# Attention followed by a max-out MoE on one core: unchained token transposes, a new query layout, one PSUM bank per job kind, and a token ring with a shorter tail

## The chip, the cores and the metric

The kernel runs on one core of a Trainium2 chip. The metric is device time in microseconds (us), the median of several executions. The profile is one execution with the hardware profiler; its span runs some 2 us below that same execution's time. So kernels of the same job are compared first, and small differences between jobs are treated with care.

## The reference, cut to what matters

```python
def _attn_ref(q, k, v):                       # q, k, v: (8, 8, 1152, 64)
    q_pool = q.reshape(B, H, S // 2, 2, D).mean(axis=3)
    scores = scale * np.matmul(q_pool, k.transpose(0, 1, 3, 2))
    attn = softmax(scores)                    # shortened here
    return np.matmul(attn, v)                 # (8, 8, 576, 64)

def _moe_ref(x, w1, w2, w_out):               # x: 4608 tokens x 512
    g = np.maximum(x @ w1, x @ w2)            # 1024 columns
    return g @ w_out
```

The kernel uses max(h1, h2) = h2 + relu(h1 - h2). It keeps w1 - w2 ("wd") and w2 @ w_out ("w21"). For each block of tokens it computes relu(x wd) (the "h" jobs, result in `gT`) and then x w21 + gT w_out (the "p" jobs).

## The kernel before

Two heads of a batch form a pair, and there are 32 pairs. For each pair the SP queue loads q, k and v. POOL casts k and v and pools q. TensorE (PE) forms the scores, ACT takes the exponentials (`eta`, `etb`), PE multiplies them by v, and DVE normalizes into `xnat`. After four pairs (one batch, 576 tokens) five DMA transposes put `xnat` into `xT`, and MoE work on these tokens may start.

A small planner in Python (`Plan`, with estimated costs) decides the static order of all instructions, and each engine executes its list in that order. PSUM holds three double banks for the scores and two single banks, `fb[0]` and `fb[1]` ("lanes"), for everything else.

`w` names what an operation writes, and `under` names the weights that once lay where `xT` is now written:

```python
def xtrans(b):
    for j in range(NCH + 1):
        ...
        under = [key for key, lo, hi in (("w2b", 512, 1536), ("w2T", 1536, 2560),
                                         ("w2f", 2560, NTOK))
                 if n0 < hi and lo < n0 + rows]
        op("SP", lambda e, ...: e.dma_start_transpose(
            xT[:, :, n0:n0 + rows], xnat[xs][0:rows, j, :]),
            r=[f"xn{xs}.{j}.{h}" for h in range(H)],
            w=[f"xT.{b}.{j}"] + under,        # every transpose "writes" w2f ...
            dma=f"d_x{xs}{j}", cost=0.95, mode="t")
```

Because each transpose writes the key `w2f` (or `w2T`, `w2b`), each one waits until its predecessor has landed, although they touch different columns. Loads, k transposes and stores of results share the in-order SP queue with them. A p job's bank becomes free when DVE has copied it to one of three output buffers `osb`, and such a buffer becomes free when its store has landed.

The lanes were filled without distinction:

```python
def refill():
    if q_queue and ...: return q_queue.pop(0)      # query and key transposes
    if av_queue and ...: return av_queue.pop(0)[0] # attention times v
    if w_queue and ...: return w_queue.pop(0)      # weights
    ... # then MoE; a p job only when no h job is in a lane
```

The softmax here doesn't subtract the row's maximum and nothing guards it: scores larger than these inputs give would overflow.

## Time and profile before

| what | before |
|---|---|
| median time | 435.13 us (432.31 to 435.33) |
| span of the profile | 438.0 us |
| PE busy / ACT busy | 388.1 us / 313.1 us |
| mean granted PE clock | 0.967 |
| PE waiting for an output copy (`DVE stage`) | 11.2 us in 8 waits |
| SP queue waiting for a token transpose | 47.1 us in 26 waits |

The profiled execution took 439.74 us, more than any of the three timed ones of its job and 1.7% above the fastest of them. So the sums of this trace lie on the high side.

These lines are from the page of the kernel before: busy time by engine, then the 40 slices of PE and of the granted clock in tenths, then the chain that ended last by engine and by line.

```profile
PE 388.1 (89%) x4714; PEld 205.9 (47%) x4765; DVE 152.7 (35%) x351; ACT 313.1 (71%) x365; POOL 130.4 (30%) x104
...
PE   2879969799999998799989997999869999999995
...
PEclk9999995889999999899999999999989999999999
...
PE 64%; DMA 15%; DVE 7%; ACT 6%; SPq 3%; issue 2%; POOL 1%; DVEq 0%
```

PE is the engine that is nearly always busy, and the chain runs mostly through it. But 15% of the chain is DMA, which should be hidden. (The loads of weights number 4765 and the matmul records 4714: some 50 matmuls are missing from this trace, so PE busy is a little too low. PE busy is therefore not compared to better than some us.)

The window table of the kernel before shows where PE stands still. Its columns are the stretch, its length, busy time of PE, weight loads, DVE, ACT and POOL (with counts), granted clock, DMA share and GB/s.

```profile
60.00:70.00 10.00, 5.41 (x34) 1.74 (x32) 6.20 (x8) 4.16 (x5) 1.32 (x2) 0.72 1.10 222
170.00:180.00 10.00, 6.48 (x88) 4.28 (x90) 1.75 (x3) 4.24 (x5) 0.00 (x0) 0.85 0.70 184
280.00:290.00 10.00, 9.73 (x139) 5.47 (x139) 4.74 (x11) 9.31 (x12) 4.71 (x4) 1.00 1.07 274
310.00:320.00 10.00, 6.59 (x54) 2.26 (x52) 0.69 (x1) 7.23 (x9) 4.08 (x3) 1.00 1.06 311
320.00:330.00 10.00, 8.61 (x126) 5.99 (x127) 4.50 (x11) 4.38 (x5) 4.07 (x3) 0.83 1.14 274
```

A good window (280 to 290) has PE at 9.7 and ACT at 9.3 of 10 us. A hole (310 to 320) has PE at 6.6, and the window after it a clock of 0.83.

The chain of the kernel before, in order of time, around that hole (start, length, what; a few entries are left out at the dots):

```profile
295.37 2.43 DMA xT<-xnat
297.79 0.01 issue
297.81 2.43 DMA xT<-xnat
...
300.26 2.40 DMA xT<-xnat
302.66 0.02 issue
302.68 4.47 DMA xT<-xnat
307.15 0.02 issue
307.16 1.17 SPq L435
...
310.01 2.31 SPq L256
...
313.05 6.94 DMA out_dram<-stage
...
320.09 0.70 DVE stage L587
320.79 0.05 issue
320.83 3.37 PE fb L333 x63
```

Read it downwards. The transposes go one after the other. Behind them in the SP queue come the loads, a k transpose and at last a store. When the store has landed, DVE may copy the next output. Only then is a PSUM bank free and PE goes on with attention, after 4.24 us of standing still. The 63 matmuls that follow take 3.37 us where the same 63 take 2.08 us at 161.67 us. Two lines of PE's timeline show it:

```profile
161.67 2.08 PE L333 MATMUL fb<-vE,eta 128*128 128x65 bf16 x63 [0.53 <-DVE stage L587]
320.83 3.37 PE L333 MATMUL fb<-vE,eta 128*128 128x65 bf16 x63 [4.24 <-DVE stage L587]
```

The clock had been halved: the window table gives 0.50 from 321 to 323 us. The Trainium skill (TensorE: Matmul & The Clock Gate, Part 1) says that an idle window of about 3.4 us halves it, and this hole agrees.

The waits of PE and of the SP queue on it (total us, times, longest):

```profile
PE fb L333 <- DVE stage L587: 11.2, 8, 4.2
...
PE sps L394 <- ACT eta L406: 6.1, 15, 0.7
PE sps L394 <- DMA kT<-kbf: 3.9, 1, 3.9
PE fb L541 <- DVE rc L357: 3.7, 7, 0.9
PE fb L571 <- DVE rc L357: 3.1, 5, 1.2
```

```profile
SPq L435 <- DMA xT<-xnat: 47.1, 26, 8.2
```

### The profile page before, as it was taken

What the parts mean: (1) busy time and instruction counts of PE and PEld (TensorE: products, weight loads), DVE (VectorE), ACT (ScalarE), POOL (GpSimd) and SP (SyncE); (2) the same over time, 40 slices, a digit from 0 to 9 for tenths busy, and PEclk for the clock granted to TensorE, in tenths of its full rate; (3) what the DMA queues carried; (4) which work ended last, traced back from release to release, by engine and by line L of the source; (5) the groups of instructions that cost most, each with busy time, mean ns of one, the idle gap of its engine ahead of it and who ended that gap; (6) DMA issues with size and microseconds to landing.
All of it is one profiled execution on the core that took longest, in us unless ns stands there. A gap on an engine that the chain in (4) does not pass through costs nothing.

```text
span 438.0 us, 10776 instructions
## 1 busy us (share of the span) xinstructions
PE 388.1 (89%) x4714; PEld 205.9 (47%) x4765; DVE 152.7 (35%) x351; ACT 313.1 (71%) x365; POOL 130.4 (30%) x104
## 2 busy tenths in 40 slices
PE   2879969799999998799989997999869999999995
PEld 1446535544554442555455554554345454633442
DVE  2246443234334412334243331442235233443121
ACT  1999948979897988499929995898829977601121
POOL 3733425265303451333045404450244201000000
PEclk9999995889999999899999999999989999999999
DMA  8999999899749994997599839982899634023213
GB/s 233 306 350 341 256 290 255 158 304 277 136 93 250 268 262 80 257 280 146 128 323 238 206 79 313 294 211 49 207 283 281 117 87 124 3 48 102 49 48 96
DMA packets 83648, 85.74 MB, mean 196 GB/s; under 512 B 54417, under 2 KB 54417, under 8 KB 83601
## 3 DMA queue, kind: packets, MB, share of 16 engines
q1 hardware_dynamic: 83600, 85.05, 78.0%
q8 instruction: 37, 0.61, 0.6%
q14 instruction: 11, 0.08, 0.1%
HBM read 62.91 MB, written 9.44 MB: 165 GB/s over the span
## 4 chain that ended last, share of the span: by engine, by line
PE 64%; DMA 15%; DVE 7%; ACT 6%; SPq 3%; issue 2%; POOL 1%; DVEq 0%
PE fb L571 17%; PE fb L333 15%; PE sps L394 13%; PE fb L541 13%; ACT eta L406 6%; DMA xT<-xnat 4%; DMA kT<-kbf 4%; PE fb L344 4%; DMA qraw<-in_q_dram 3%; DMA out_dram<-stage 3%; DVE stage L555 2%; DVE xnat L361 2%; DVE stage L587 1%; SPq L256 1%; SPq L435 1%
## 5 line engine op out<-in xcount | busy, mean ns | idle before, releaser
L406 ACT ACTIVATE eta<-sps 128x1024 bf16<-128x1024 f32 x288 | 270.1, 1051 | 62.6 <-PE sps L394 62.1
L394 PE MATMUL sps<-qpT,kT 64*128 64x64 bf16 (+1 forms) x1152 | 108.0, 298 | 12.5 <-ACT eta L406 6.1
L333 PE MATMUL fb<-vE,eta 128*128 128x65 bf16 x2304 | 97.0, 199 | 11.9 <-DVE stage L587 11.2
L333 PEld LDWEIGHTS fb<-vE,eta 128*128 128x128 bf16 x2304 | 86.5, 101 | 37.8 <-DVE stage L587 12.4
L249 POOL TENSOR_SCALAR kbf<-kraw 128x1152 bf16<-128x1152 f32 x31 | 35.7, 1150 | 159.7 <-DMA kraw<-in_k_dram 159.7
L541 PE MATMUL fb<-xT,wd 128*128 128x512 bf16 x259 | 68.8, 384 | 6.6 <-DVE rc L357 3.7
L262 POOL TENSOR_TENSOR qp<-qraw 96x768 bf16<-96x768 f32 x32 | 57.8, 1806 | 46.8 <-DMA qraw<-in_q_dram 37.0
L571 PE MATMUL fb<-wo,stage 128*128 128x512 bf16 x281 | 70.7, 380 | 0.9 <-issue 0.8
L555 DVE TENSOR_SCALAR stage<-fb 128x512 bf16<-128x512 f32 x64 | 43.3, 689 | 56.6 <-PE fb L541 56.6
L394 PEld LDWEIGHTS sps<-qpT,kT 64*128 64x128 bf16 x1152 | 30.5, 95 | 66.2 <-ACT eta L406 38.3
L587 DVE COPY stage<-fb 128x512 f32<-128x512 f32 x32 | 21.8, 690 | 104.5 <-PE fb L571 95.3
L418 ACT ACTIVATE etb<-sps 128x1024 bf16<-128x1024 f32 x64 | 39.2, 678 | 10.6 <-PE sps L394 10.1
L270 POOL TENSOR_SCALAR vE<-vraw 128x1152 bf16<-128x1152 f32 x32 | 36.8, 1149 | 26.0 <-PE sps L394 16.6
L571 PEld LDWEIGHTS fb<-wo,stage 128*128 128x128 bf16 x288 | 25.1, 98 | 36.6 <-issue 11.9
L541 PEld LDWEIGHTS fb<-xT,wd 128*128 128x128 bf16 x288 | 22.3, 98 | 37.3 <-issue 5.1
L571 PE MATMUL fb<-w,xT 128*128 128x512 bf16 x132 | 35.3, 380 | 4.3 <-DVE rc L357 3.1
L357 DVE RECIPROCAL rc<-fb 128x6 f32<-128x6 f32 (+1 forms) x64 | 12.1, 189 | 74.1 <-PE fb L344 54.9
L361 DVE TENSOR_TENSOR xnat<-fb,rc 128x256 bf16<-128x256 f32 x64 | 27.2, 425 | 2.2
L550 ACT ACTIVATE stage<-fb 128x512 bf16<-128x512 f32 x8 | 4.8, 597 | 28.2 <-PE fb L541 28.2
L344 PE MATMUL fb<-vE,etb 128*128 128x131 bf16 x288 | 22.6, 224 | 0.0
L289 PE MATMUL fb<-ident,qp 96*128 96x96 bf16 x192 | 14.6, 216 | 8.6 <-POOL qp L262 7.9
L571 PEld LDWEIGHTS fb<-w,xT 128*128 128x128 bf16 x144 | 11.4, 97 | 21.9 <-DVE xnat L373 4.1
(27 smaller groups left out, 109.0 us busy)
## 6 DMA issues: line engine op xcount, KB each, us to landing
qraw<-in_q_dram SPq DMA_DIRECT2D x32, 576.0 KB, 9.4
kraw<-in_k_dram SPq DMA_DIRECT2D x32, 576.0 KB, 7.5
vraw<-in_v_dram SPq DMA_DIRECT2D x32, 576.0 KB, 10.3
out_dram<-stage SPq DMA_DIRECT2D x24, 192.0 KB, 3.2
out_dram<-stage SPq DMA_DIRECT2D x24, 128.0 KB, 4.3
xT<-in_moe_w_dram SPq DMA_DIRECT2D x1, 2048.0 KB, 15.6
stage<-in_moe_w_out_dram SPq DMA_DIRECT2D x1, 2048.0 KB, 22.3
stage<-in_moe_w_dram SPq DMA_DIRECT2D x1, 2048.0 KB, 21.9
```

What stands on the lines that cost most here:

```text
L249: op("DVE" if i == 0 else "POOL", lambda g: g.tensor_scalar(kbf[s][:, :, :, :].rearrange("p t h d -> p h t d"), kraw[s][:, :, :, :], 1.0, ...
L262: op("POOL", lambda g: g.tensor_tensor(qp[s][:, :, :, :].rearrange("p u h d -> p h u d"), qraw[s][:, :, :, 0, :], qraw[s][:, :, :, 1, :], ...
L270: op("POOL", lambda g: g.tensor_scalar(vE[v3][:, :, :, 0:D].rearrange("p t h d -> p h t d"), vraw[s][:, :, :, :], 1.0, 1.0, ALU.mult, ALU. ...
L333: last = e.matmul(fb[m][:, sb * 66:sb * 66 + 65], eta[es][:, half, t, sb * P:(sb + 1) * P], vE[vs][:, t, half, 0:65], start=(t == 0), stop ...
L344: last = e.matmul(fb[m][:, 4 * 66:4 * 66 + 131], etb[es][:, t, :, :].rearrange("p h c -> p (h c)"), vE[vs][:, t, :, :].rearrange("p h c -> ...
L361: dve(lambda e: e.tensor_tensor(xnat[xs][:, 0:NCH, c:c + D], a[:, 0:NCH * 66].rearrange("p (j c) -> p j c", c=66)[:, :, 0:D], rc[half][:, ...
L394: return e.matmul(sps[r][:, half, col:col + n], kT[ks][h:h + 64, t, :], qpT[qs][h:h + 64, lo:lo + n], start=True, stop=True)
L406: return e.activation(eta[es][:, :, g, :], sps[r][:, :, :], EXP, scale=scale)
L418: return e.activation(etb[es][:, t0:t0 + n, :, :].rearrange("p t h c -> p h t c"), sps[r][:, :, 0:n * NB].rearrange("p h (t c) -> p h t c" ...
L541: last = e.matmul(fb[m][:, :], wd[:, ct, ft * P:(ft + 1) * P], xT[:, ct, n0:n0 + 512], start=(ct == 0), stop=(ct == NC_ - 1))
L555: dve(lambda e: e.tensor_scalar_max(gT[gs][:, ft, :], fb[m][:, :], 0.0), [f"f{m}"], [f"gT{gs}.{ft}", f"f{m}"], 0.63)
L571: last = e.matmul(fb[m][:, :], lhs, rhs, start=(j == 0), stop=(j == NC_ + NF - 1))
```

## The change

Its intent is to take DMA off the chain, to give attention and MoE a bank each, and to shorten the part that depends on the last batch. The diff is long; these are its parts, cut to the core.

1. Token transposes wait for the old users of their place, but no longer count as writers of it:

```diff
-                    w=[f"xT.{b}.{j}"] + under,
-                    dma=f"d_x{xs}{j}", cost=0.95, mode="t")
+                    w=[f"xT.{b}.{j}"], after=under,
+                    dma=f"d_x{xs}{j}", cost=0.65, mode="t")
```

2. Queries arrive as 128 rows of 4608 B and POOL pools them in two halves of 64 partitions. The raw buffers are three instead of two, and loads run one pair further ahead:

```diff
-        qraw = [sbuf([QP, 2, QU, 2, D], FP32, f"qraw{s}") for s in range(2)]   # QP = 96
+        qraw = [sbuf([P, QU, 2, D], FP32, f"qraw{s}") for s in range(3)]       # QP = 64
...
-                q[b, h0:h0 + 2, :, :].rearrange("h (p r) d -> p h (r d)", p=QP)),
+                q[b, h0:h0 + 2, :, :].rearrange("h (p r) d -> (h p) (r d)", p=QP)),
...
+            for half in range(2):
+                a = qraw[r][half * QP:half * QP + QP, :, :, :]
+                op("POOL", ... qp[s][:, :, half, :], a[:, :, 0, :], a[:, :, 1, :], ALU.add ...)
...
-                load_k(i + 3); load_q(i + 3)      # and load_v(i + 2)
+                load_k(i + 4); load_q(i + 4)      # and load_v(i + 3)
```

3. Bank 0 takes queries and attention first, bank 1 weights and MoE; h and p jobs of different blocks may overlap:

```diff
+            if kk == 0:
+                if q_queue and ...: return q_queue.pop(0)
+                if av_queue and ...: return av_queue.pop(0)[0]
+            more_moe()
             if w_queue and ...: return w_queue.pop(0)
+            job = (take_h() or take_p()) if kk == 0 else (take_p() or take_h())
```

4. `gT` becomes a ring of 1024 token columns, and the blocks end where the last batch begins:

```diff
+        hblocks = [(0, 448)] + [(448 + 512 * j, 960 + 512 * j) for j in range(7)]
+        hblocks += [(4032, 4320), (4320, 4608)]
+        tiles = [(0, 64)] + [(64 + P * j, 64 + P * j + P) for j in range(35)] + [(4544, 4608)]
```

The dependent tail shrinks from 1024 to 576 tokens; the output tiles become 37 (two of them half) instead of 36.

More of the change, by code (lines that the diff above doesn't have):

```diff
@@ L30, in __init__, with deps @@
         self.mode = None
-    def deps(self, r, w):
+        self.last = {}
+    def deps(self, r, w, after=()):
         raw = {self.writer[k] for k in r if k in self.writer}
         deps = set(raw)
-        for k in w:
+        for k in tuple(w) + tuple(after):
             if k in self.writer:
@@ L39, in deps, with when @@
         return deps, raw
-    def when(self, eng, r=(), w=()):
+    def when(self, eng, r=(), w=(), after=()):
         t = self.free.get(eng, 0.0)
-        for d in self.deps(r, w)[0]:
+        for d in self.deps(r, w, after)[0]:
             p = self.ops[d]
@@ L48, in when, with op @@
         return t
-    def op(self, eng, fn, r=(), w=(), dma=None, cost=0.1, mode="f"):
+    def op(self, eng, fn, r=(), w=(), dma=None, cost=0.1, mode="f", after=(), solo=False):
         n = len(self.ops)
-        deps, raw = self.deps(r, w)
-        t = self.when(eng, r, w)
+        deps, raw = self.deps(r, w, after)
+        prev = self.last.get(eng)
+        if prev is not None and (solo or self.ops[prev]["solo"]):
+            deps.add(prev)
+            raw.add(prev)
+        self.last[eng] = n
+        t = self.when(eng, r, w, after)
         if dma is not None:
@@ L64, in op @@
         self.ops.append(dict(eng=eng, fn=fn, deps=deps, raw=raw, dma=dma, w=tuple(w),
-                             seen=seen, end=self.free[eng]))
+                             seen=seen, end=self.free[eng], solo=solo))
         for k in r:
@@ L135, with __init__ @@
 class Job:
-    def __init__(self, kind, units, evac, done=None):
+    def __init__(self, kind, units, evac, done=None, nb=None):
         self.kind, self.units, self.evac, self.done = kind, units, evac, done
+        self.nb = nb
 def bass_funnel_attn__then__act_maxout2_kernel(
@@ L156, in bass_funnel_attn__then__act_maxout2_kernel @@
     NT = S // P
-    QP = 96
+    QP = 64
     QU = SQ // QP
@@ L167, in bass_funnel_attn__then__act_maxout2_kernel @@
     NBLK = NTOK // 512
-    assert D == 64 and S == NT * P and SQ == QP * QU and C == H * D and E == 512
+    assert D == 64 and S == NT * P and SQ == QP * QU and QU == NT and C == H * D and E == 512
     assert NB == 64 and NTOK % 512 == 0 and NT == 9
@@ L180, in bass_funnel_attn__then__act_maxout2_kernel @@
         ident = sbuf([P, P], BF16, "ident")
-        qraw = [sbuf([QP, 2, QU, 2, D], FP32, f"qraw{s}") for s in range(2)]
-        kraw = [sbuf([P, 2, NT, D], FP32, f"kraw{s}") for s in range(2)]
-        vraw = [sbuf([P, 2, NT, D], FP32, f"vraw{s}") for s in range(2)]
+        qraw = [sbuf([P, QU, 2, D], FP32, f"qraw{s}") for s in range(3)]
+        kraw = [sbuf([P, 2, NT, D], FP32, f"kraw{s}") for s in range(3)]
+        vraw = [sbuf([P, 2, NT, D], FP32, f"vraw{s}") for s in range(3)]
         qp = [sbuf([QP, QU, 2, D], BF16, f"qp{s}") for s in range(2)]
@@ L203, in bass_funnel_attn__then__act_maxout2_kernel @@
         g16 = stage[:, 0:NC_ * F].bitcast(BF16)
-        gT = [g16[:, s * NF * 512:(s + 1) * NF * 512].rearrange("p (f n) -> p f n", f=NF)
-              for s in range(2)]
+        gT = g16.rearrange("p (f n) -> p f n", f=NF)
         osb = [stage[:, NC_ * F + s * E:NC_ * F + (s + 1) * E] for s in range(3)]
@@ L226, in load_k @@
         def load_k(i):
-            b, h0, s = i // NHP, 2 * (i % NHP), i % 2
+            b, h0, s = i // NHP, 2 * (i % NHP), i % 3
             op("SP", lambda e: e.dma_start(
@@ L230, in load_k @@
                 k[b, h0:h0 + 2, :, :].rearrange("h (p t) d -> p h (t d)", t=NT)),
-                w=[f"kraw{s}"], dma=f"d_k{s}", cost=1.8)
+                w=[f"kraw{s}"], dma=f"d_k{s}", cost=1.7)
         def load_q(i):
-            b, h0, s = i // NHP, 2 * (i % NHP), i % 2
+            b, h0, s = i // NHP, 2 * (i % NHP), i % 3
             op("SP", lambda e: e.dma_start(
-                qraw[s][:, :, :, :, :].rearrange("p h u r d -> p h (u r d)"),
-                q[b, h0:h0 + 2, :, :].rearrange("h (p r) d -> p h (r d)", p=QP)),
-                w=[f"qraw{s}"], dma=f"d_q{s}", cost=2.1)
+                qraw[s][:, :, :, :].rearrange("p u r d -> p (u r d)"),
+                q[b, h0:h0 + 2, :, :].rearrange("h (p r) d -> (h p) (r d)", p=QP)),
+                w=[f"qraw{s}"], dma=f"d_q{s}", cost=1.55)
         def load_v(i):
-            b, h0, s = i // NHP, 2 * (i % NHP), i % 2
+            b, h0, s = i // NHP, 2 * (i % NHP), i % 3
             op("SP", lambda e: e.dma_start(
@@ L244, in load_v @@
                 v[b, h0:h0 + 2, :, :].rearrange("h (p t) d -> p h (t d)", t=NT)),
-                w=[f"vraw{s}"], dma=f"d_v{s}", cost=1.8)
+                w=[f"vraw{s}"], dma=f"d_v{s}", cost=1.7)
         def cast_k(i):
-            s = i % 2
+            s, r = i % 2, i % 3
             op("DVE" if i == 0 else "POOL", lambda g: g.tensor_scalar(
-                kbf[s][:, :, :, :].rearrange("p t h d -> p h t d"), kraw[s][:, :, :, :],
-                1.0, 1.0, ALU.mult, ALU.mult), r=[f"kraw{s}"], w=[f"kbf{s}"], cost=1.13)
+                kbf[s][:, :, :, :].rearrange("p t h d -> p h t d"), kraw[r][:, :, :, :],
+                1.0, 1.0, ALU.mult, ALU.mult), r=[f"kraw{r}"], w=[f"kbf{s}"], cost=1.13)
         def ktrans(i):
@@ L260, in cast_q, with unit @@
         def cast_q(i):
-            s = i % 2
-            op("POOL", lambda g: g.tensor_tensor(
-                qp[s][:, :, :, :].rearrange("p u h d -> p h u d"),
-                qraw[s][:, :, :, 0, :], qraw[s][:, :, :, 1, :], ALU.add),
-                r=[f"qraw{s}"], w=[f"qp{s}"], cost=1.77)
+            s, r = i % 2, i % 3
+            for half in range(2):
+                a = qraw[r][half * QP:half * QP + QP, :, :, :]
+                op("POOL", lambda g, half=half, a=a: g.tensor_tensor(
+                    qp[s][:, :, half, :], a[:, :, 0, :], a[:, :, 1, :], ALU.add),
+                    r=[f"qraw{r}"], w=[f"qp{s}.{half}"], cost=1.4,
+                    solo=half == 1)
         def cast_v(i):
-            s = i % 2
-            v3 = i % 3
+            r = i % 3
             op("POOL", lambda g: g.tensor_scalar(
-                vE[v3][:, :, :, 0:D].rearrange("p t h d -> p h t d"), vraw[s][:, :, :, :],
-                1.0, 1.0, ALU.mult, ALU.mult), r=[f"vraw{s}"], w=[f"vE{v3}"], cost=1.13)
-        def unit(r, cost, go):
+                vE[r][:, :, :, 0:D].rearrange("p t h d -> p h t d"), vraw[r][:, :, :, :],
+                1.0, 1.0, ALU.mult, ALU.mult), r=[f"vraw{r}"], w=[f"vE{r}"], cost=1.13)
+        def unit(r, cost, go, mode="f"):
             def plan_it(m):
-                op("PE", lambda e: go(e, m), r=r, w=[f"f{m}"], cost=cost)
+                op("PE", lambda e: go(e, m), r=r, w=[f"f{m}"], cost=cost, mode=mode)
             return r, plan_it, cost
@@ L297, in evac @@
                     [f"f{m}"], [f"qpT{s}", f"f{m}"], 0.4)
-            return Job("q", [unit([f"qp{s}", "ident"], 0.26, go)], evac, ("q", i))
+            return Job("q", [unit([f"qp{s}.0", f"qp{s}.1", "ident"], 0.3, go, "s")], evac, ("q", i))
         def ktrans_pe(i):
@@ L434, in xtrans @@
                          if n0 < hi and lo < n0 + rows]
+                if "w2T" in under:
+                    under += [f"w2T{ct}" for ct in range(NC_)]
                 op("SP", lambda e, rows=rows, n0=n0, j=j: e.dma_start_transpose(
@@ L507, in go @@
                         return last
-                    return unit([f"w2T{ct}", "wo", "w2T"], 0.432, go)
+                    return unit([f"w2T{ct}", "wo"], 0.432, go)
                 def evac(m, ct=ct):
@@ L517, in bass_funnel_attn__then__act_maxout2_kernel, with store, gcol @@
         held = {}
-        def store(t, s):
-            n0, n1 = t * P, (t + 1) * P
-            n = n0
-            while n < n1:
-                b, c = n // SQ, n % SQ
-                u, p0 = c // QP, c % QP
-                ln = min(n1 - n, QP - p0)
-                op("SP", lambda e, n=n, b=b, u=u, p0=p0, ln=ln: e.dma_start(
-                    out[b * SQ:(b + 1) * SQ, :].rearrange("(p u) e -> u p e", u=QU)[
-                        u, p0:p0 + ln, :],
-                    osb[s][n - n0:n - n0 + ln, :]), r=[f"osb{s}"], dma=f"d_o{s}",
-                    cost=0.7 * ln / P)
-                n += ln
+        def store(n0, n1, s):
+            for n in range(n0, n1, QP):
+                b, u = n // SQ, n % SQ // QP
+                op("SP", lambda e, n=n, b=b, u=u: e.dma_start(
+                    out[b * SQ:(b + 1) * SQ, :].rearrange("(p u) e -> u p e", u=QU)[u, :, :],
+                    osb[s][n - n0:n - n0 + QP, :]), r=[f"osb{s}"], dma=f"d_o{s}", cost=0.4)
+        def gcol(n):
+            return (n + 64) % 1024
         def moe_jobs(nb, tail):
-            n0 = nb * 512
-            gs = nb % 2
+            n0, n1 = hblocks[nb]
+            size = n1 - n0
+            g0 = gcol(n0)
             jobs = []
@@ L541, in go @@
                             last = e.matmul(
-                                fb[m][:, :], wd[:, ct, ft * P:(ft + 1) * P],
-                                xT[:, ct, n0:n0 + 512],
+                                fb[m][:, 0:size], wd[:, ct, ft * P:(ft + 1) * P],
+                                xT[:, ct, n0:n1],
                                 start=(ct == 0), stop=(ct == NC_ - 1))
                         return last
-                    return unit(["wd"] + xkeys(n0, n0 + 512), 0.432, go)
+                    return unit(["wd"] + xkeys(n0, n1), 0.432 * size / 512, go)
                 def evac(m, ft=ft):
@@ L550, in evac, with part @@
                         op("ACT", lambda e: e.activation(
-                            gT[gs][:, ft, :], fb[m][:, :],
+                            gT[:, ft, g0:g0 + size], fb[m][:, 0:size],
                             mybir.ActivationFunctionType.Relu),
-                            r=[f"f{m}"], w=[f"gT{gs}.{ft}", f"f{m}"], cost=0.55)
+                            r=[f"f{m}"], w=[f"gT.{g0 // 64}.{ft}", f"f{m}"],
+                            cost=0.12 + size / 1200.0)
                     else:
                         dve(lambda e: e.tensor_scalar_max(
-                            gT[gs][:, ft, :], fb[m][:, :], 0.0),
-                            [f"f{m}"], [f"gT{gs}.{ft}", f"f{m}"], 0.63)
-                jobs.append(Job("h", [part(0), part(1)], evac))
-            for nt in range(4):
-                c0 = n0 + nt * P
-                def part(kk, nt=nt, c0=c0):
+                            gT[:, ft, g0:g0 + size], fb[m][:, 0:size], 0.0),
+                            [f"f{m}"], [f"gT.{g0 // 64}.{ft}", f"f{m}"], 0.1 + size / 960.0)
+                jobs.append(Job("h", [part(0), part(1)], evac, nb=nb))
+            for lo, hi in tiles:
+                if not n0 < hi <= n1:
+                    continue
+                def part(kk, lo=lo, hi=hi):
                     def go(e, m):
@@ L565, in go, with evac @@
                             if j < NC_:
-                                lhs, rhs = xT[:, j, c0:c0 + P], w21[:, j, :]
+                                lhs, rhs = xT[:, j, lo:hi], w21[:, j, :]
                             else:
                                 ft = j - NC_
-                                lhs = gT[gs][:, ft, nt * P:(nt + 1) * P]
+                                lhs = gT[:, ft, gcol(lo):gcol(lo) + hi - lo]
                                 rhs = wo[:, ft, :]
-                            last = e.matmul(fb[m][:, :], lhs, rhs,
+                            last = e.matmul(fb[m][0:hi - lo, :], lhs, rhs,
                                             start=(j == 0), stop=(j == NC_ + NF - 1))
                         return last
-                    rd = (["w21"] + xkeys(c0, c0 + P)) if kk < 2 else (
-                        ["wo", f"gT{gs}.{2 * kk - 4}", f"gT{gs}.{2 * kk - 3}"])
+                    rd = (["w21"] + xkeys(lo, hi)) if kk < 2 else (
+                        ["wo"] + [f"gT.{g}.{ft}" for ft in (2 * kk - 4, 2 * kk - 3)
+                                  for g in gkeys(lo, hi)])
                     return unit(rd, 0.432, go)
-                def evac(m, nt=nt):
+                def evac(m, lo=lo, hi=hi):
                     o = ocount[0] % 3
@@ L582, in evac, with gkeys @@
                         store(*held.pop(o))
-                    if tail and nt % 2:
-                        op("ACT", lambda e: e.copy(osb[o][:, :], fb[m][:, :]),
+                    if tail and ocount[0] % 2:
+                        op("ACT", lambda e: e.copy(osb[o][0:hi - lo, :], fb[m][0:hi - lo, :]),
                            r=[f"f{m}"], w=[f"osb{o}", f"f{m}"], cost=0.55)
                     else:
-                        dve(lambda e: e.tensor_copy(osb[o][:, :], fb[m][:, :]),
+                        dve(lambda e: e.tensor_copy(osb[o][0:hi - lo, :], fb[m][0:hi - lo, :]),
                             [f"f{m}"], [f"osb{o}", f"f{m}"], 0.63)
-                    held[o] = (nb * 4 + nt, o)
-                jobs.append(Job("p", [part(kk) for kk in range(6)], evac))
-            return jobs
+                    held[o] = (lo, hi, o)
+                jobs.append(Job("p", [part(kk) for kk in range(6)], evac, nb=nb))
+            return jobs
+        def gkeys(lo, hi):
+            return sorted({gcol(n0) // 64 for n0, n1 in hblocks if n0 < hi and lo < n1})
         NG = NT + 2
@@ L603, in bass_funnel_attn__then__act_maxout2_kernel @@
         w_queue = []
-        moe_queue = []
-        blocks = [((512 * (nb + 1) - 1) // SQ, nb) for nb in range(NBLK)]
+        h_queue = []
+        p_queue = []
+        h_open = {}
+        p_left = [0]
+        hblocks = [(0, 448)] + [(448 + 512 * j, 960 + 512 * j) for j in range(7)]
+        hblocks += [(4032, 4320), (4320, 4608)]
+        tiles = [(0, 64)] + [(64 + P * j, 64 + P * j + P) for j in range(35)] + [(4544, 4608)]
+        tile_end = {nb: sum(1 for lo, hi in tiles if hi <= n1) for nb, (n0, n1) in enumerate(hblocks)}
+        blocks = [((n1 - 1) // SQ, nb) for nb, (n0, n1) in enumerate(hblocks)]
         q_done = set()
         k_done = set()
-        KPE = 5
+        K_PE = (0, 1, 2, 3, 4)
         W_AT = (0, 1, 3)
@@ L625, in start_k @@
             cast_k(i)
-            if i < KPE:
+            if i in K_PE:
                 q_queue.extend(ktrans_pe(i))
@@ L637, in enter @@
                 q_queue.append(qtrans(i + 1))
+            if i + 4 < NPAIR:
+                load_k(i + 4)
+                load_q(i + 4)
             if i + 3 < NPAIR:
-                load_k(i + 3)
-                load_q(i + 3)
-            if i + 2 < NPAIR:
-                load_v(i + 2)
+                load_v(i + 3)
             if i in W_AT:
@@ L676, in av_open, with more_moe @@
             return nxt >= at and plan.when("PE", r=job.units[0][0]) <= now() + 0.1
-        def refill():
-            if q_queue and plan.when("PE", r=q_queue[0].units[0][0]) <= now():
-                return q_queue.pop(0)
-            if av_queue and (av_open() or nxt >= len(groups)):
-                return av_queue.pop(0)[0]
+        def more_moe():
+            while blocks and blocks[0][0] in x_done:
+                nb = blocks[0][1]
+                tail = nxt >= len(groups)
+                if nb - p_left[0] >= 2:
+                    return
+                if not tail and plan.when("PE", r=xkeys(*hblocks[nb])) > now():
+                    return
+                jobs = moe_jobs(nb, tail)
+                h_queue.extend((job, nb) for job in jobs[:NF])
+                p_queue.extend((job, nb) for job in jobs[NF:])
+                blocks.pop(0)
@@ new lines, in take_h, with take_p, refill @@
+        def take_h():
+            if h_queue and h_queue[0][1] - p_left[0] < 2:
+                job, nb = h_queue.pop(0)
+                h_open[nb] = h_open.get(nb, NF) - 1
+                return job
+        def take_p():
+            if p_queue:
+                nb = p_queue[0][1]
+                if h_open.get(nb, NF) == 0 and not any(l and l.kind == "h" and l.nb == nb for l in lane):
+                    return p_queue.pop(0)[0]
+        def refill(kk):
+            if kk == 0:
+                if q_queue and plan.when("PE", r=q_queue[0].units[0][0]) <= now():
+                    return q_queue.pop(0)
+                if av_queue and (av_open() or nxt >= len(groups)):
+                    return av_queue.pop(0)[0]
+            more_moe()
@@ L684, in refill @@
             if w_queue and plan.when("PE", r=w_queue[0].units[0][0]) <= now():
                 return w_queue.pop(0)
-            if not moe_queue and blocks and blocks[0][0] in x_done:
-                nb = blocks[0][1]
-                if plan.when("PE", r=xkeys(nb * 512, nb * 512 + 512)) <= now() or nxt >= len(groups):
-                    moe_queue.extend(moe_jobs(blocks.pop(0)[1], nxt >= len(groups)))
-            if moe_queue:
-                if moe_queue[0].kind == "p" and any(l and l.kind == "h" for l in lane):
-                    return None
-                return moe_queue.pop(0)
@@ L694, in refill @@
-            return None
+            job = (take_h() or take_p()) if kk == 0 else (take_p() or take_h())
+            if job is None and kk == 1 and av_queue and (av_open() or nxt >= len(groups)):
+                return av_queue.pop(0)[0]
+            return job
         def burst_now(size):
@@ L718, in nxt_of, with behind @@
             return (p + 1) * NG + g
+        def behind():
+            done = 9 * len(av_half) / 2.0 + (4 - len(lane[0].units) if lane[0].kind == "a" else 0)
+            return done < 9 * (nxt / NG - 1.0) + 1.5
         def emit_burst(todo_g):
@@ L728, in emit_burst @@
                     a0, a1 = av_jobs(p)
-                    av_queue.extend([(a0, nxt_of(p, 1)), (a1, nxt_of(p, 6))])
+                    av_queue.extend([(a0, nxt_of(p, 0)), (a1, nxt_of(p, 5))])
             nxt += len(todo_g)
+            if q_queue and q_queue[0].done and q_queue[0].done[0] == "q":
+                for kk in (0, 1):
+                    if lane[kk] is None and plan.when(
+                            "PE", r=q_queue[0].units[0][0], w=[f"f{kk}"]) <= now() + 0.05:
+                        lane[kk] = q_queue.pop(0)
+                        emit_unit(kk)
+                        break
         def emit_unit(kk):
@@ L742, in emit_unit @@
                         av_done.add(len(av_half) // 2 - 1)
+                if job.kind == "p":
+                    p_count[0] += 1
+                    p_left[0] = sum(1 for nb in tile_end if tile_end[nb] <= p_count[0])
                 if job.done:
@@ L746, in bass_funnel_attn__then__act_maxout2_kernel @@
         av_half = []
+        p_count = [0]
         setup()
@@ L761, in bass_funnel_attn__then__act_maxout2_kernel @@
         load_v(1)
+        load_k(3)
+        load_q(3)
+        load_v(2)
         turn = 0
-        while nxt < len(groups) or av_queue or moe_queue or blocks or any(lane) or x_wait:
+        while nxt < len(groups) or av_queue or h_queue or p_queue or blocks or any(lane) or x_wait:
             flush()
@@ L773, in bass_funnel_attn__then__act_maxout2_kernel @@
                 if lane[kk] is None:
-                    lane[kk] = refill()
+                    lane[kk] = refill(kk)
             best = None
@@ L778, in bass_funnel_attn__then__act_maxout2_kernel @@
                     t = plan.when("PE", r=lane[kk].units[0][0], w=[f"f{kk}"])
-                    if best is None or t < best[0] - 0.02:
+                    if best is None or t < best[0] - 0.02 or (
+                            kk == 0 and lane[0].kind == "a" and t <= now() + 0.02 and behind()):
                         best = (t, kk, t + lane[kk].units[0][2] - now())
```

## The prediction

> **What bounds the kernel now.** TensorE, in order. The busy table gives PE 388.1 us of the 438.0 us traced (89%), ACT 313.1, POOL 130. In undisturbed 10 us windows (280-290, 330-340) PE is busy 9.7 and ACT 9.3 us. About 50 us of PE idle remain: 8 before the first matmul, 5 after the last, the rest in holes of the window table: 60-70 (PE 5.4), 80-90 (7.5), 170-180 (6.5), 260-280 (8.0, 8.6), 310-330 (6.6, 8.6). PE's waits: output copy (DVE stage) 11.2 us, 8 times, up to 4.2; reciprocal of the attention result 6.8; eta/etb 7.4; kT transposed by DMA 3.9; pooled queries 7.9 (start only).
>
> The 4 us holes have one story in the chain of waits: DMA xT<-xnat, 2.5 us, three to five in a row, then the SP queue, out_dram, the output copy, the attention matmuls. A batch's five token transposes share a write key (w2f, w2T), so each waits for the one before: SP waits 47.1 us for xT<-xnat, and one batch holds the in-order SP queue for 10 to 19 us. Stores stand behind, the three output buffers fill, a p job keeps its PSUM bank, attention cannot start.
>
> **What the change does.**
> 1. Transposes wait on `after` instead of writing the shared key: 5 x 1.2 us of issue instead of 10 to 19. Most of the 11.2 us goes, and the slow clock after those holes (0.83-0.85 in 170-180, 270-280, 320-330), about 4 us. Estimate -14.
> 2. Bank 0 for attention first, bank 1 for MoE, h and p jobs overlapping: most of rc's 6.8 us and some h/p idling. -6.
> 3. Third raw buffers, one pair more prefetch; q as 128 rows of 4608 B instead of 192 of 3072 B. POOL waits 37 us for q and 160 us for k, off the chain except around 36-65 us (kT 17.5, q 9.4 us), where three 2 MB weight loads keep DMA over 100% busy. More prefetch adds load there; the hole at 60-90 (5 us idle, clock 0.72-0.77) shrinks only partly: -4.
> 4. Tail: the last batch becomes 2x288 tokens, not two blocks of 512 at 17.9 us. The tail is 49 us (384 to 433), but PE is 99% busy there; moving work earlier gains only what earlier holes take: -3.
> 5. Costs. One more p tile, 12 x 0.216 us = +2.6. POOL adds two 64x576 halves: 1806 ns / 768 x 576 = 1.36 us each, 2.7 against 1.81, with a wait between; POOL is 30% busy, so only +1 at the start. The Trainium skill (GPSIMD Engine Reference, section 3.1) puts a two-input add at about 2.6 cycles per element; the trace's 2.35 ns agrees roughly. Nine small query transposes for six, without a mode change: 0.
>
> Sum: -27 + 3.6, about -24.
>
> **Predicted: 411 us, 8 in 10 between 400 and 424.** Faster by over 2%: 0.86; within 2%: 0.11; slower: 0.03. PE busy stays at 385-390; only idle goes.
>
> **Right or wrong in the profile.** PE's wait for the output copy under 3 us; SP's for xT<-xnat near 0; windows near 9.7 PE outside the start; mean clock 0.98; POOL TENSOR_TENSOR x64 near 1.36 us; 35-42 us after the last exponential rather than 53. The Trainium skill (TensorE: Matmul & The Clock Gate, Part 1) says idle windows of about 3.4 us halve the clock; the dips here follow 4 us holes.
>
> **What would make it wrong.** DMA bound below the surface (share over 1.0 in half the windows): faster pairs wait for kT or k. One attention bank makes its halves wait for each other's evacuation (1.1 us of DVE). The 60-90 hole grows. Better: attention reaches ACT's pace, 400.

## More of the kernel before

The kernel before took 435 to 439 us as a median in four jobs (the chips of three are recorded, and differ), and single executions of it spread from 431 to 442 us.

## The result

The changed kernel took 418.01 us (416.41 to 418.57), where the kernel before took 435.23 us in the runs of both. The ratio is 0.960, with a 95% interval of 0.953 to 0.967. A later control on another chip gave 416.11 against 434.54 us, ratio 0.959.

The page of the changed kernel, the same lines as before:

```profile
PE 379.6 (91%) x4846; PEld 203.6 (49%) x4905; DVE 156.3 (38%) x355; ACT 314.4 (76%) x370; POOL 164.9 (40%) x136
...
PE   0787897899999999999999999999999999999996
...
PEclk9988998999999999999999999999999999999999
...
PE 80%; DVE 8%; ACT 6%; issue 2%; DMA 1%; POOL 1%; another core or an unknown queue 0%
```

The holes in the middle are gone, DMA has left the chain (15% to 1%), and the mean clock rose from 0.967 to 0.987. (Between executions of the kernel before the mean clock ranged from 0.961 to 0.990, so the size of that rise is uncertain.) The start (the first eight slices) is no better.

The windows of the changed kernel, in the form used above; the last three are its tail:

```profile
60.00:70.00 10.00, 7.66 (x102) 3.81 (x100) 8.38 (x10) 9.57 (x12) 4.61 (x3) 1.00 0.89 229
170.00:180.00 10.00, 9.52 (x142) 5.14 (x142) 4.14 (x10) 9.52 (x12) 5.06 (x4) 1.00 1.07 384
...
310.00:320.00 10.00, 9.69 (x147) 5.43 (x145) 3.44 (x9) 9.81 (x12) 1.16 (x1) 1.00 0.33 62
...
342.00:380.00 38.00, 36.93 (x233) 16.57 (x237) 13.90 (x24) 2.39 (x4) 0.00 (x0) 1.00 0.31 65
380.00:400.00 20.00, 18.38 (x102) 9.50 (x103) 4.29 (x9) 3.82 (x8) 0.00 (x0) 1.00 0.32 68
400.00:416.00 16.00, 12.32 (x62) 5.59 (x60) 2.27 (x4) 2.40 (x5) 0.00 (x0) 0.98 0.34 71
```

PE's waits in the changed kernel that answer to those above. The output copy is down from 11.2 us to below 2; the reciprocal's 6.8 us became about 6 us of waits for the next step of the same normalization (`xnat`), below and in some smaller lines. The SP queue's list no longer holds a wait for xT<-xnat.

```profile
PE sps L403 <- ACT eta L415: 5.5, 10, 0.7
PE fb L342 <- DVE xnat L382: 3.1, 7, 0.8
PE fb L342 <- DVE xnat L370: 2.0, 1, 2.0
...
PE fb L581 <- DVE stage L598: 1.4, 5, 0.3
```

The last exponential shows what became of the gain. These are the last ACT rows of the two timelines, before and after (start, length):

```profile
378.71 1.19 ACT L418 ACTIVATE etb<-sps 128x1024 bf16<-128x1024 f32 x2
```

```profile
340.52 1.20 ACT L427 ACTIVATE etb<-sps 128x1024 bf16<-128x1024 f32 x2
```

Attention now ends 38 us earlier. Yet the span fell by 22 us only (the medians by 17), because the stretch after it grew from 58 to 74 us. PE has the same work to do. Whatever MoE does not fit beside attention is done after it, with PE busy at 97% (36.93 of 38 us).

### The profile page after: what moved, and what is told of

The parts are those of the page before. It is cut to its first block, busy times and chain, and to the rows that moved or that the text cites. A ratio compares the mean times of both kernels' runs of the same rounds, so it can differ in the third digit from the quotient of the medians.

```text
span 415.9 us, 11123 instructions
## 1 busy us (share of the span) xinstructions
PE 379.6 (91%) x4846; PEld 203.6 (49%) x4905; DVE 156.3 (38%) x355; ACT 314.4 (76%) x370; POOL 164.9 (40%) x136
## 4 chain that ended last, share of the span: by engine, by line
PE 80%; DVE 8%; ACT 6%; issue 2%; DMA 1%; POOL 1%; another core or an unknown queue 0%
PE fb L581 23%; PE fb L342 17%; PE sps L403 17%; PE fb L549 15%; ACT eta L415 5%; PE fb L353 4%; PE fb L298 2%; DVE wd L488 2%; PE fb L516 1%; DVE stage L598 1%; DMA qraw<-in_q_dram 1%; DVE xnat L370 1%; DVE xnat L382 1%; DVE wo L483 1%; POOL qp L272 1%
## 5 line engine op out<-in xcount | busy, mean ns | idle before, releaser
L272 POOL TENSOR_TENSOR qp<-qraw 64x576 bf16<-64x576 f32 x64 | 90.8, 1419 | 60.9 <-PE fb L298 54.2
L549 PE MATMUL fb<-xT,wd 128*128 128x512 bf16 (+2 forms) x304 | 76.3, 358 | 3.1 <-issue 1.3
L581 PE MATMUL fb<-wo,stage 128*128 128x512 bf16 (+1 forms) x275 | 76.5, 380 | 1.7 <-issue 1.0
L564 DVE TENSOR_SCALAR stage<-fb 128x512 bf16<-128x512 f32 (+2 forms) x68 | 44.4, 656 | 69.4 <-PE fb L549 69.0
L366 DVE RECIPROCAL rc<-fb 128x6 f32<-128x6 f32 x64 | 12.1, 189 | 114.0 <-PE fb L353 71.7
L581 PEld LDWEIGHTS fb<-wo,stage 128*128 128x128 bf16 (+1 forms) x296 | 26.0, 98 | 30.3 <-issue 7.4
L581 PE MATMUL fb<-w,xT 128*128 128x512 bf16 (+1 forms) x130 | 37.3, 381 | 3.3 <-DVE stage L598 1.4
L598 DVE COPY stage<-fb 128x512 f32<-128x512 f32 (+1 forms) x32 | 22.1, 690 | 31.4 <-PE fb L581 31.1
L298 PE MATMUL fb<-ident,qp 64*128 64x64 bf16 x288 | 14.0, 192 | 9.8 <-POOL qp L272 8.8
L298 PEld LDWEIGHTS fb<-ident,qp 64*128 64x128 bf16 x288 | 10.7, 96 | 19.6 <-POOL qp L272 8.8
```

Source lines behind the costliest of these rows:

```text
L272: op("POOL", lambda g, half=half, a=a: g.tensor_tensor(qp[s][:, :, half, :], a[:, :, 0, :], a[:, :, 1, :], ALU.add), r=[f"qraw{r}"], w=[f" ...
L298: last = e.transpose(mb[:, u * QP:(u + 1) * QP], qp[s][:, u, :, :].rearrange("p h d -> p (h d)"), ident[0:QP, 0:QP])
L549: last = e.matmul(fb[m][:, 0:size], wd[:, ct, ft * P:(ft + 1) * P], xT[:, ct, n0:n1], start=(ct == 0), stop=(ct == NC_ - 1))
L564: dve(lambda e: e.tensor_scalar_max(gT[:, ft, g0:g0 + size], fb[m][:, 0:size], 0.0), [f"f{m}"], [f"gT.{g0 // 64}.{ft}", f"f{m}"], 0.1 + si ...
L581: last = e.matmul(fb[m][0:hi - lo, :], lhs, rhs, start=(j == 0), stop=(j == NC_ + NF - 1))
```

## The experiments

Theories, as named in the expectations: T1, the unchained transposes are most of the gain. T2, the bank policy is. T3, the query load and buffers are. T4 (added after the first job): PE bounds the kernel, so the other parts cancel. T5: the short tail is worth something. The twelve kernels all gave correct results.

| run | edit | median us | ratio to before | 95% |
|---|---|---|---|---|
| b_after | before + part 1 alone | 418.28 | 0.955 | 0.949 to 0.961 |
| a_under | changed, part 1 undone | 434.56 | 0.993 | 0.987 to 0.999 |
| a_lanes | changed, banks open | 415.90 | 0.950 | 0.945 to 0.955 |
| a_raw2 | changed, two raw buffers | 423.17 | 0.968 | 0.961 to 0.975 |
| a_q96 | changed, old query path | 426.04 | 0.969 | 0.963 to 0.975 |
| a_moe512 | changed, equal blocks | 412.48 | 0.938 | 0.933 to 0.943 |
| a_align | changed, short tail, 36 tiles | 414.95 | 0.946 | 0.940 to 0.953 |
| best1 | four edits at once | 419.04 | 0.953 | 0.948 to 0.959 |
| after_ctl | changed, unaltered | 416.11 | 0.959 | 0.955 to 0.964 |
| b_q128 | b_after + new query path | 424.05 | 0.977 | 0.973 to 0.982 |
| b_q3 | b_q128 + third buffers | 421.70 | 0.971 | 0.967 to 0.976 |
| best2 | a_lanes + a_moe512 | 415.37 | 0.958 | 0.954 to 0.961 |

The first four ran in one job (before: 437.90 us), the next four in another (439.16), the last four in a third (434.54).

### b_after: part 1 alone

The edit is the first diff above, applied to the kernel before (with `after` added to the planner, and with the weight jobs and transposes depending on the keys `w2T0` to `w2T3` in place of `w2T` alone).

> The kernel before with one part of the change: token transposes wait on the old users of their place (after=) and no longer chain on a shared write key. Theory T1 (the unchained transposes are most of the gain): 420 to 425 us, the PE wait for the output copy under 3 us (before 11.2), the SP wait for xT<-xnat near 0 (before 47.1), mean clock about 0.98. Rival T2 (bank policy and h/p overlap are most of it): 430 to 434 us. Rival T3 (third raw buffers and the query load): 430 to 434 us.

It took 418.28 us, which is the whole gain. T1's three signs came true: PE's waits for the output copy fell from 11.2 to

```profile
PE fb L333 <- DVE stage L589: 1.7, 10, 0.2
```

the SP queue has no wait for xT<-xnat in its list, and the clock is 0.986. (DMA still makes up 14% of this kernel's chain, now mostly loads and k transposes of the first 64 us. So that share alone does not measure the gain.) T2 and T3 as explanations of the net gain fall. One thing stays mixed: the edit also tells the planner that tokens come earlier. In the two traces PE's weight loads come in the same order only up to about 80 us, and after that in another one. So the gain belongs to the edit as a whole. Between its first and last matmul PE was idle for 37.4 us before and 18.0 us here, worked out from the two traces (the records missing from the first make its figure a little too high). About half of that drop is the wait for the output copy. How much of the gain comes from shorter waits on the chip, and how much from the new order, was not told apart.

### a_under: part 1 undone

```diff
-                    w=[f"xT.{b}.{j}"], after=under,
-                    dma=f"d_x{xs}{j}", cost=0.65, mode="t")
+                    w=[f"xT.{b}.{j}"] + under,
+                    dma=f"d_x{xs}{j}", cost=0.95, mode="t")
```

> The changed kernel with the shared write key put back, so a batch's transposes chain again; all else changed. T1: 428 to 433 us, with 4 us PE waits for the output copy back and the clock near 0.97. T2 or T3: 416 to 421 us, because the new order or deeper buffers absorb the blocked SP queue.

At 434.56 us the gain is gone, as T1 said. But the signature that I had expected, 4 us waits for the output copy, did not come: no wait for `DVE stage` is over 0.5 us. The SP queue does wait again for the transposes, 26 times as before. The first line below is from a_under's list of SP waits, the second from its window table (clock 0.72):

```profile
SPq L446 <- DMA xT<-xnat: 36.5, 26, 2.7
```

```profile
220.00:230.00 10.00, 6.55 (x38) 2.20 (x37) 2.38 (x6) 8.91 (x10) 1.82 (x2) 0.72 0.98 321
```

Its timeline shows PE there with score matmuls only, one pair for each exponential, and then MoE at half clock (0.50 from 225 to 231 us). No single wait in this stretch is over 0.69 us. PE was busy for 1.6 of the 4 us from 220 to 224, and that was enough for the clock to fall:

```profile
220.71 0.39 PE L403 MATMUL sps<-qpT,kT 64*128 64x512 bf16 x2 [0.69 <-ACT eta L415]
221.63 0.39 PE L403 MATMUL sps<-qpT,kT 64*128 64x512 bf16 x2 [0.53 <-ACT eta L415]
...
226.75 4.99 PE L549 MATMUL fb<-xT,wd 128*128 128x512 bf16 x12
```

By estimate, twelve such matmuls at the full clock take about 2.6 us (12 x 0.216, from rows of six that take 1.47 us). So putting the chain back costs 14 us by the ratios (0.993 against 0.960) or 16.5 to 18.5 us by the medians of different jobs, near the 19.6 us that taking it away gained in the old order; but the cost lies in a different place. In the old order PE waits for a bank. In the new one the static order has no MoE work ready beside the scores. The edit changes both the waits on the chip and the times that the planner assumes (tokens come later), so these two effects of the chain were not told apart.

### a_lanes: both banks open

```diff
-            if kk == 0:
-                if q_queue and ...
-                if av_queue and ...
+            if q_queue and ...
+            if av_queue and ...
...
-            job = (take_h() or take_p()) if kk == 0 else (take_p() or take_h())
+            return take_h() or take_p()
```

> The changed kernel with both PSUM banks open to every job again (queries, attention, weights, then MoE), and no preference for bank 0; the token ring stays. T1: 417 to 421 us, the policy is worth under 1%. T2: 426 us or more, the PE waits for the reciprocal (6.8 us before) are back and the exponentials lose their 10.0 us per pair. In both cases the start may be 1 to 2 us quicker, since query and key transposes then use two banks.

415.90 us: the policy that gives each kind a bank gains nothing, and perhaps costs up to 1%. Attention ended at 333.9 us here, 8 us earlier than in the changed kernel (332.71 plus 1.19 in its timeline), and the total hardly moved. Three kernels whose last exponential ended at 333.9 us (here), 341.7 us (the changed kernel) and 358.8 us (b_after) took 415.9, 418.0 and 418.3 us. That fits the PE bound: in these three the end of attention hardly moved the total.

### a_raw2: two raw buffers

```diff
-        kraw = [... for s in range(3)]      # q and v alike
+        kraw = [... for s in range(2)]
...
-                load_k(i + 4); load_q(i + 4)
+                load_k(i + 3); load_q(i + 3)
```

This kernel also counts finished halves before it transposes a batch: in its order the last half of a batch may finish before the one ahead of it.

> The changed kernel with two raw buffers and the old load distances (and a count of finished halves in place of the last half as the sign that a batch is done, which it needs to stay correct). T3: 426 us or more, POOL waits for k and q are on the chain. T1 and T2: 416 to 421 us, with POOL idle for q and k as before but off the chain; the first 85 us no slower than with three buffers.

423.17 us, 5 to 7 us above the changed kernel (418.01 and 416.11, both of other jobs). The result lies between the two expectations. By the ratios (0.968 against 0.960) the third buffers are worth just under 1% (some 4 us) inside the changed kernel, and the intervals overlap. The trace is on T3's side: POOL waited 104.1 us for k here against 0.5 us in the changed kernel, and from 40 to 60 us ACT was busy 13.4 instead of 19.2 us, so the first 85 us did become slower.

### a_q96: the old query path

```diff
-    QP = 64
+    QP = 96
...
-            for half in range(2): ...
+            op("POOL", ... qraw[r][:, :, :, 0, :], qraw[r][:, :, :, 1, :], ALU.add ...)
```

> The changed kernel with the old query path: 192 rows of 3072 B into 96 partitions, one POOL addition of 1.81 us for each pair of heads instead of two of 1.42, six query transposes instead of nine, stores cut at 96 tokens. Theory T4 (PE bound, the query path is off the chain except at the start): 416 to 420 us, the first matmul about 1 us earlier (7.9 instead of 8.8 us). Rival T3 (the query load relieves the DMA engines): 423 us or more.

426.04 us, which T3 had right. T4's sign at the start came true (first matmul at 7.72 instead of 8.84 us), its total did not. The worth of the query path in the changed kernel is 8 to 10 us by medians of different jobs, but only about 4 us by the ratios (0.969 against 0.960), whose intervals overlap. In the same job a_align, the changed kernel with one tile less, was 11 us faster. The edit also changes POOL's work (132 instead of 165 us) and the stores, so it isn't the load alone. The packet records of the traces show what the load itself gains. This table is the mean time of a packet by its size, worked out over the whole trace:

```
kernel   3072 B (q)      4608 B (q)      2304 B (k, v)
before   186 ns          -               117 ns
after    -               191 ns          104 ns
a_q96    186 ns          -               119 ns
```

A query packet of 4608 B takes hardly longer than one of 3072 B. By estimate one pair's queries keep 16 engines busy for 128 x 191 / 16 = 1.53 us instead of 192 x 186 / 16 = 2.23 us. The Trainium skill (SBUF — State Buffer, "Door 1: The DMA port swizzle") has a reason that fits: 96 partitions put twice as many rows on half of the 16 ports, so those ports take two thirds of the bytes. By an estimate from that page the load then takes 4/3 of a balanced one; the trace shows 2.23 / 1.53 = 1.46. No run here varies the partitions alone.

### a_moe512: equal blocks of 512 tokens

```diff
-        hblocks = [(0, 448)] + [...] + [(4032, 4320), (4320, 4608)]
-        tiles = [(0, 64)] + [...] + [(4544, 4608)]
+        hblocks = [(512 * j, 512 * j + 512) for j in range(9)]
+        tiles = [(P * j, P * j + P) for j in range(36)]
```

> The changed kernel with nine equal blocks of 512 tokens and 36 output tiles, so the last two blocks (1024 tokens) need the last batch instead of 576 tokens. T4 (PE bound: 72 us of MoE are left over after the last exponential, so a short dependent tail buys nothing, and the 37th tile costs 12 x 0.216 = 2.6 us): 414 to 417 us. Rival T5 (the short tail is worth something): 420 us or more.

412.48 us: the short tail costs time, and this is the fastest kernel, below the changed kernel by 3.6 and 5.5 us against its two medians (its slowest run, 412.82, is below the fastest of the changed kernel's ten, 414.57). The windows of its tail:

```profile
339.00:380.00 41.00, 39.93 (x246) 17.66 (x247) 16.10 (x27) 2.39 (x4) 0.00 (x0) 1.00 0.29 60
380.00:400.00 20.00, 19.89 (x91) 8.31 (x92) 4.84 (x7) 3.56 (x6) 0.00 (x0) 1.00 0.31 66
400.00:411.00 11.00, 6.85 (x32) 2.86 (x30) 1.38 (x2) 1.17 (x2) 0.00 (x0) 1.00 0.45 95
```

With 512-token blocks PE is busy 19.89 of 20 us between 380 and 400; with 288-token blocks it was 18.38, a loss of 1.5 us. The thirty-seventh tile adds 2.6 us. Together that is 4.1 us by estimate, about the difference. The next run, of the same job, separates the two: it has the short blocks and 36 tiles, took 414.95 us, and so puts the short blocks (with the longer ring that they need there) at 2.5 us (its fastest run, 414.42, is above the slowest here). Since some 70 us of PE work stand after the last exponential anyway, a dependent tail of 1024 tokens hides as well as one of 576.

### a_align: the short tail with 36 tiles

```diff
-            return (n + 64) % 1024
+            return n % 1536           # a longer ring, so tiles stay aligned at 128
...
+        hblocks = [(512 * j, 512 * j + 512) for j in range(7)]
+        hblocks += [(3584, 4032), (4032, 4320), (4320, 4608)]
+        tiles = [(P * j, P * j + P) for j in range(36)]
```

> The changed kernel with the same short last blocks (288 and 288 tokens) but a ring of 1536 token columns, so that output tiles stay aligned at 128 and are 36 instead of 37. T4: 415 to 416 us, 2.6 us less than the changed kernel. If the half tiles cost nothing: 418 us.

414.95 us. That is between the changed kernel and a_moe512, as T4 says of the tile, but the step (1.2 to 3.1 us against the two medians of the changed kernel) is near the scatter between jobs.

### best1: four edits at once

```diff
+            return n % 1536                                    # aligned tiles
+            return take_h() or take_p()                        # both banks open
+                eng = "DVE" if i == 0 and half else "POOL"     # first query sum
+                    later(("w2b", "wo", "wd")[n], lambda: ready(ct + 1))  # casts one by one
```

> An attempt at a better kernel: both banks open to every job, 36 aligned output tiles, the second half of the first query sum on DVE beside POOL, and the weight casts handed to DVE one by one instead of four in a row (the four subtractions took 6.5 us in a row and PE waited 2 us for an attention result behind them). T4: 408 to 412 us: 415.9 of the open banks, less 2.6 for the tile, 1.8 for the start, 0 to 3 for the casts.

A miss: 419.04 us. The early start worked (the first `etb` exponential began at 18.94 us instead of 20.52 in a_lanes), but PE was busy only 18.6 of 20 us in several middle windows, where a_lanes had 20.0 (120 to 180 us). The planner laid the middle out differently. The edit also puts the first query sum ahead of the first k cast and holds MoE back until `wd` is cast. So many edits at once do not tell which did it. In the same job a_align, which shares the aligned tiles and short blocks, was 4 us faster, so the loss comes with one of the other edits or with the order that they led to.

### after_ctl, b_q128, b_q3, best2

after_ctl is the changed kernel unaltered.

> The changed kernel unaltered, as a control on this chip: the kernel before has been 435 to 439 us in three jobs, so only the ratio carries over. Expected ratio 0.96 (418 us where before is 435, 421 where it is 439).

It gave 416.11 us, ratio 0.959, as expected. b_q128 adds the new query path to b_after:

```diff
-    QP = 96
+    QP = 64       # load, two POOL halves and nine transposes as in the changed kernel
```

> The kernel before, with the unchained transposes and the new query path (128 rows of 4608 B, pooled in two halves), two raw buffers and the old order. T3 (the query load relieves the DMA engines, as its return to the old form cost the changed kernel some 8 us): ratio 0.935 to 0.945. T4 (PE bound, the query path is worth nothing by itself): the ratio of the unchained transposes alone, 0.955, within 0.005.

Neither theory: ratio 0.977. The same query path that was worth 4 to 10 us inside the changed kernel costs about 2% in the old order (0.977 here against 0.955 for b_after in another job; the intervals are apart). The windows from 30 to 60 us, b_after first, then b_q128:

```profile
30.00:60.00 30.00, 28.85 (x435) 17.41 (x434) 16.14 (x36) 28.20 (x33) 12.57 (x9) 0.95 1.12 299
```

```profile
30.00:60.00 30.00, 23.16 (x309) 15.16 (x309) 16.88 (x26) 21.05 (x26) 16.38 (x12) 0.77 1.01 320
```

PE loses 5.7 us there and the clock falls to 0.77. Its chain of waits goes through DVE casting w_out, 6.25 us for four casts. These are the groups of that cast, b_after first (busy us, mean ns):

```profile
L474 DVE CAST wo<-stage 128x1024 bf16<-128x1024 f32 x4 | 2.5, 686 | 0.7 <-DMA stage<-in_moe_w_out_dram 0.7
```

```profile
L482 DVE CAST wo<-stage 128x1024 bf16<-128x1024 f32 x4 | 6.3, 1643 | 0.0
```

The cast did not change; POOL beside it did (16.4 instead of 12.6 us busy in the window). The Trainium skill (SBUF — State Buffer, "SBUF: two separate sides") says DVE and GpSimd share a pair of ports that one holds for a whole instruction. The traces agree with it: 686 ns became 1643 ns on average. Taken one by one, they show more. In the traces of b_after, after, b_q128 and a_q96 these kernels' 32 casts of `wo` and of w2 split cleanly: the 21 that began while no POOL instruction ran took 0.67 to 0.70 us, and the 11 that began during one ended 0.54 to 0.56 us after that instruction did. No run takes POOL's work away, and that the lost 5.7 us all come from this is not shown. Attention results wait behind those casts on DVE, and PE waits for them.

b_q3 adds the third raw buffers to b_q128 (the diff of a_raw2 in reverse).

> The same with the third raw buffers and one pair more of prefetch: the whole change less its scheduling (banks, ring, short tail). T3: ratio 0.93 to 0.945. T4: 0.95 to 0.96. If it is below the control, the scheduling part of the change costs time.

Ratio 0.971, outside both ranges. The transposes, the query path and the buffers without the new order are slower than the transposes alone. So the scheduling part does gain when the new query path is there: 0.959 against 0.971 in the same job. But it does no better than the old order with the old query path (b_after, 0.955).

best2 opens the banks and uses equal blocks.

```diff
+            return take_h() or take_p()                        # as in a_lanes
+        hblocks = [(512 * j, 512 * j + 512) for j in range(9)]  # as in a_moe512
```

> The changed kernel with both banks open to all jobs and with nine equal blocks of 512 tokens: the two edits that each did better than the changed kernel. If they add: ratio 0.925 to 0.932. If both remove the same idle time: 0.937 to 0.94.

A miss: 0.958, no better than the control. The two edits don't add; by its ratio the result is worse than a_moe512 alone (0.938). The fastest version remains a_moe512.

## Why the prediction was right or wrong

The time came out inside the range (418.0 and 416.1 against 400 to 424), and the direction was right. The size was too large, 24 us forecast and 17 to 18 measured, and the split over the parts was wrong. That the sum still came out inside the range is in part luck: term 1 was some 5 us too small, and terms 2 to 4 booked 13 us that together came to about nothing. Point by point:

1. **Transposes, -14.** The mechanism was right and the term too small: alone they gave 19.6 us (437.90 to 418.28), and undone they took 14 to 18.5 us back (434.56 us, against the changed kernel by ratio and by medians). The 11.2 us of waits and the slow clock were counted; the rest was not. The "4 us holes" that halve the clock were single waits of 3.01, 2.75 and 4.24 us.
2. **Banks, -6.** Wrong. The reciprocal's waits moved on to `xnat`, and with the banks open again the kernel was no slower (415.90; ratio 0.950 against 0.960).
3. **Buffers and query load, -4 net.** Wrong as a number of its own: it depends on the order. In the changed kernel the third buffers are worth 4 to 7 us and the query path 4 to 10 (less by ratios, more by medians of different jobs); in the old order the query path costs about 2%.
4. **Tail, -3.** Wrong in sign. I expected 35 to 42 us from the last exponential to the last output copy, instead of 53; it was about 71 (341.72 to 413.16 us). I had written that PE was 99% busy in the tail and that moved work gains only what holes can take, and then still booked a gain.
5. **Costs, +3.6.** The parts were right: the first matmul at 8.8 instead of 7.9 us, POOL halves of 1.42 us (forecast 1.36). The tile's 2.6 us agree with the 1.2 to 3.1 us between a_align and the changed kernel, which is near the scatter. What was missing is that POOL, "30% busy", slows DVE: four subtractions of weights took 1.69 us each on average instead of 1.22, and PE waited 2.0 us for an attention result behind them.

The step that failed is the sum. Terms 2 to 4 were added as if each were free PE time. Once term 1 had filled the holes, PE was nearly always busy, and the other parts mostly exchanged one wait for another. They sum to about zero: 0.955 with part 1 alone, 0.959 to 0.960 with everything. That the sum is zero is measured; that PE's bound is the reason fits the traces but was not tested apart from the planner's new order. What stays open is why single edits of the order move the time by 1 to 2% in either direction (best1, best2). The planner lays out every instruction anew for each edit, and no run holds the order fixed.

## What to carry to other kernels

Look for dependencies that the program declares but does not have: a shared name in a write list cost this kernel 14 to 20 us, through an in-order queue, three output buffers and a PSUM bank. When one engine is nearly always busy, an earlier end of one phase shows up as a longer next phase, so cost a change by the idle time of that engine that it removes, not by the phase it shortens. Test the parts of a large change alone and in reverse, because here one part had opposite signs in two orders.

## What the Trainium skill lacked or had wrong

- SBUF — State Buffer, "Door 1: The DMA port swizzle": its table of measured loads has no row for 96 partitions. Here 192 rows of 3072 B to 96 partitions took 186 ns a packet and 128 rows of 4608 B to 128 partitions 191 ns, so 1.46 times the engine time for the same bytes.
- SBUF — State Buffer, "SBUF: two separate sides": it gives the lock between DVE and GpSimd, but no durations of casts or subtractions under it. Here a 128x1024 DVE cast went from 686 to 1643 ns on average beside POOL work (11 delayed casts ended 0.54 to 0.56 us after the POOL instruction), and a 128x1024 DVE subtraction from 1219 to 1690 ns.
- GPSIMD Engine Reference, section 3.1: nothing wrong found. It gives about 2.6 cycles per element for an add of two inputs, 2.2 ns at its clock of 1.2 GHz. Here fp32 adds took 1806 ns for 768 elements (2.35 ns) and 1419 ns for 576 (2.46 ns), start cost included.
- TensorE: Matmul & The Clock Gate, Part 1: it ties the halved clock to an idle window of about 3.4 us. A hole of 4.24 us agrees, but single waits of 3.01 and 2.75 us were followed by the same dip (clock 0.83 to 0.85 over 10 us). In a_under the clock fell to 0.50 with no wait over 0.69 us, after 4 us in which PE was busy 1.6 us. So a sparse stretch was enough; an idle one was not needed.
